# PSUM after the token loop: one rotating pool of four slots, against four one-slot pools with a written order in which the first and third slot change places

## The chip, the cores and the metric

The kernel runs on one core of a Trainium2 chip. The metric is device time in microseconds, the median of the timed runs. All time marks are microseconds from the first instruction of the profiled execution. Engines are named as in the profile: PE multiplies matrices, PEld is its weight load, DVE, ACT and POOL are the vector, scalar and GpSimd engines, and SP issues most of the DMAs.

## The reference

One transformer block on x of 2048 tokens by 640 values, in bfloat16: linear attention with a learned softmax feature map (32 heads of 20 values), then a gated feed-forward of width 1536.

```python
# _A_ref on layernorm(x)
phi_q = concat([softmax(pq), softmax(-pq)]);  phi_k = concat([softmax(pk), softmax(-pk)])
kv  = einsum("bhsf,bhsd->bhfd", phi_k, v);    z = einsum("bhsf->bhf", phi_k)
o   = einsum("bhqf,bhfd->bhqd", phi_q, kv) / (einsum("bhqf,bhf->bhq", phi_q, z) + 1e-6)
h   = x + o @ wo
# _B_ref on layernorm(h)
h2  = h + (gelu(hn @ w_gate) * (hn @ w_up)) @ w_down
```

## The kernel before

The 2048 tokens are 16 tiles of 128. The kernel has three stretches.

**The token loop** (`for t in range(NT)`, L463). For each tile PE makes keys and values, ACT takes exponentials, DVE and POOL normalise, and `kv_tile` (L345) adds the tile's part of the state into one PSUM tile, `kvp`. From the fourth tile on, PSUM has a pool of three two-bank slots (`psG`, L466) and a fourth two-bank slot for `kvp` (`psK`, L467). In the last turn of the loop `q_mm(0)` to `q_mm(3)` (L365) make the first four groups of queries, `q_exp` (L377) turns each into two exponentials on ACT, and the last `kv_tile` calls follow at L516 and L517. `kv_mask` (L356) then copies `kvp` into `KV` on DVE.

**The transition** (L518 to L802). The old pools are closed and `psG2` is opened at L523: one pool of four slots, each two banks of PSUM, so that slot 0 is banks 0 and 1, slot 1 is banks 2 and 3, slot 2 is banks 4 and 5, slot 3 is banks 6 and 7. Every PSUM tile of this stretch comes from it through `gtile` (L104) or, for the transposes on PE, straight from `transpose_to` (L152). The first calls are `q_mm(4, (0,))` (L758, five matmuls of the next query group), `attn_a(0, 1)` (L759, attention numerators and denominators of tile 0, two PSUM tiles `ab`), and so on. PE's and SP's order is the order of the calls, and so is that of the other engines (`manual_schedule`, L77 and L78).

**The feed-forward** (L805 to L829). `weave` (L739) runs the list of `gate_up` and `down` calls of one quarter of the tokens and puts stages of the remaining attention tiles between them. `gate_up` (L688) makes the gate and up products of 128 hidden columns in one two-bank tile `gu`; ACT takes the gelu of the first bank into `g` (L700), and DVE multiplies the second bank by it into `GT` (L703). `down` (L705) multiplies 12 such `GT` tiles by `Wd` into `pd` (L716), and DVE adds the residual into `y`. The first quarter is done in two halves. In the second half, at step 12 of the weave, that is after the twelfth `gate_up` and before the first `down`, `split()` (L543) closes `psG2` and opens `psB`, a pool of eight one-bank slots, which serves to the end.

A tile of a new pool may be written when all readers of the tiles that held its banks are done (`reuse_waits="tile"`). The waits are laid on PE's matmuls and weight loads.

Slots around the two borders, as the built program has them:

| tile | made at | slot before |
|---|---|---|
| query groups 0, 1, 2, 3, in the loop | L374 | 0, 2, 1, 0 (of the old pool) |
| kvp, in the loop | L352 | 3 (its own pool) |
| query group 4, first tile of `psG2` | L374 | 0 |
| the two `ab` tiles of attention tile 0 | L565 | 3, 2 |
| last `po` tile of `psG2` (attention tile 7) | L637 | 0 |
| `gu` of the tenth, eleventh and twelfth `gate_up`, the last tiles of `psG2` | L697 | 1, 3, 2 |
| first two tiles of `psB`, both `pd` | L716 | bank 0, bank 7 |

Of the kernel before, what the change touches and what calls it, by code (L numbers as in the profile page):

```python
# [8 lines left out]
BF16 = mybir.dt.bfloat16  # L9
F32 = mybir.dt.float32  # L10
# [3 lines left out]
PSUM = bass.MemoryType.PSUM  # L14
# [3 lines left out]
def kernel(  # L18
# [13 lines left out]
    P = 128  # L32
# [42 lines left out]
    ps_cm = ExitStack()  # L75
    psG = ps_cm.enter_context(tc.tile_pool(name="psG0", bufs=4, space=PSUM, reuse_waits="tile"))
# [24 lines left out]
    def small(pool, shape, name, bufs=3):  # L101
        return pool.tile(shape, F32, name=name, bufs=bufs)

    def gtile(name):  # L104
        return psG.tile([P, 2, 512], F32, name=name, tag="G")

    def ln_stats(pool, tiles, tag, act=True, between=None, log=False):

# [43 lines left out]
    def transpose_to(dst, src, on_pe, on_dve=False):  # L152

        if on_pe:
            tp = psG.tile([P, 16, P], BF16, name="tp", tag="G")
            for c in range(NC):
                nc.tensor.transpose(tp[:, c, :], src[:, c * P:(c + 1) * P], ident)  # L157
            (nc.vector.tensor_copy if on_dve else nc.scalar.copy)(dst, tp[:, 0:NC, :])  # L158
        else:
            nc.sync.dma_start_transpose(dst, src)  # L160
# [47 lines left out]
    for c in range(NC):  # L208
# [4 lines left out]
                                compare_op=ALU.is_ge, fill=0.0, base=Dh - 1 - off, channel_multiplier=-1)  # L213

    wu = gtile("wu")
    def warm(*cols):
        for n in cols:
# [4 lines left out]
    def fold(WT, W2, quarters, ds=range(NC)):  # L222


        n, w = (2, QF) if quarters else (1, HD)
        runs = []
        for c in range(NC):
            lo, hi = H0[c] * Dh, (H0[c] + NH[c]) * Dh
            for r in range(2 * n):
                a, b = max(lo, r * w), min(hi, (r + 1) * w)  # L230
                if a < b:
                    runs.append((r // n, r, c, a, b))
        runs.sort()
        for d in ds:
            wa = gtile("wa")
            wr = wa.rearrange("p u (q x) -> p (u q) x", q=n)
            for i, (u, r, c, a, b) in enumerate(runs):
                nc.tensor.matmul(wr[:, r, a - r * w:b - r * w], lhsT=WT[:, c, d * P:(d + 1) * P],
                                 rhs=BD[:, c].rearrange("p a b -> p (a b)")[:, a - H0[c] * Dh:b - H0[c] * Dh],
                                 start=(i == 0 or runs[i - 1][0] != u),  # L240
                                 stop=(i + 1 == len(runs) or runs[i + 1][0] != u), skip_group_check=True)
            dst, src = W2[:, d, :].rearrange("p (u f) -> p u f", u=2), wr[:, :, 0:w]
            if quarters:
                dst = W2[:, d, :].rearrange("p (c r f) -> p r c f", c=NC, r=4)
                src = src.rearrange("p r (c f) -> p r c f", c=NC)
            if d in (QA if quarters else KA):
                nc.scalar.copy(dst, src)
            else:
                nc.vector.tensor_copy(dst, src)
# [19 lines left out]
    def ln_ap(t, on_act=False, on_pe=False):  # L269
        ln = (ln_act if on_act else ln_dve)(p1, "1", *lnp[t])  # L270
        if on_pe:
            lnp[t] = ln
        else:
            transpose_to(LN1T[t // 4][:, :, t % 4 * P:(t % 4 + 1) * P], ln, False)

    def ln_tp(t, on_dve=False):
        transpose_to(LN1T[t // 4][:, :, t % 4 * P:(t % 4 + 1) * P], lnp[t], True, on_dve)
# [12 lines left out]
    def v_mm(t, us=(0, 1)):  # L290
        if 0 in us:
            pv[t] = gtile("pv")
        proj(pv[t], t, Wv, us)
# [120 lines left out]
    def tr_c(t):  # L414
        transpose_to(LN1T[0][:, :, t * P:(t + 1) * P], xc[t], True)
# [47 lines left out]
    for t in range(NT):  # L463
        if t == T3:
            ps_cm.close()
            psG = ps_cm.enter_context(tc.tile_pool(name="psG", bufs=3, space=PSUM, reuse_waits="tile"))  # L466
# [53 lines left out]
    p1_cm.__exit__(None, None, None)  # L520
    ps_cm.close()
    ps_cm = ExitStack()
    psG = ps_cm.enter_context(tc.tile_pool(name="psG2", bufs=4, space=PSUM, reuse_waits="tile"))  # L523


    p2 = ctx.enter_context(tc.tile_pool(name="p2", bufs=1, reuse_waits="tile"))
# [334 lines left out]
```

## Time and profile before

| | us |
|---|---|
| timed, median of 3 (lowest to highest) | 275.93 (275.52 to 276.19) |
| the profiled execution's own time | 276.65 |
| its span, first to last instruction | 274.7 |
| PE busy | 268.2 (98%) |
| PEld busy | 171.7 (63%) |
| DVE busy | 174.2 (63%) |
| ACT busy | 141.1 (51%) |
| POOL busy | 96.6 (35%) |

The granted clock of PE is 0.999 over the span. A row of the timeline gives the start, the length, the engine, the line, the operation, what it writes and reads, the shapes and how many instructions are merged into it; the bracket at its end is the time that the engine had nothing to run just before, and which instruction ended that. Matmuls overlap, so a row of several matmuls ends later than the next row begins. The chain of work that ended last is followed back from the last instruction, and PE has 73% of the span in it; it reaches back to 70.10 us.

### The profile page before, as it was taken

What the parts mean: (1) busy time and instruction counts of PE and PEld (TensorE: products, weight loads), DVE (VectorE), ACT (ScalarE), POOL (GpSimd) and SP (SyncE); (2) the same over time, 40 slices, a digit from 0 to 9 for tenths busy, and PEclk for the clock granted to TensorE, in tenths of its full rate; (3) what the DMA queues carried; (4) which work ended last, traced back from release to release, by engine and by line L of the source; (5) the groups of instructions that cost most, each with busy time, mean ns of one, the idle gap of its engine ahead of it and who ended that gap; (6) DMA issues with size and microseconds to landing.
All of it is one profiled execution on the core that took longest, in us unless ns stands there. A gap on an engine that the chain in (4) does not pass through costs nothing.

```text
span 274.7 us, 7230 instructions
## 1 busy us (share of the span) xinstructions
PE 268.2 (98%) x2978; PEld 171.7 (63%) x2995; DVE 174.2 (63%) x332; ACT 141.1 (51%) x241; POOL 96.6 (35%) x219
## 2 busy tenths in 40 slices
PE   7999999999899999999999999999999999999996
PEld 4776777774455887788754554675554576444574
DVE  5879999997586776675459873346976333333332
ACT  5789897787689755374534445212445510223100
POOL 4248999775012227365321552101165300000000
PEclk9999999999999999999999999999999999999999
DMA  7963637577079021323111232110214111000011
GB/s 190 221 218 71 66 60 91 78 152 312 2 246 328 5 50 37 85 51 73 33 43 49 26 70 51 40 58 1 66 32 64 35 48 50 24 0 0 2 48 48
DMA packets 42400, 21.46 MB, mean 78 GB/s; under 512 B 35200, under 2 KB 40576, under 8 KB 42368
## 3 DMA queue, kind: packets, MB, share of 16 engines
q1 hardware_dynamic: 41712, 20.98, 31.9%
q8 instruction: 23, 0.38, 0.6%
q10 hardware_dynamic: 656, 0.03, 0.2%
q14 instruction: 9, 0.07, 0.1%
HBM read 10.18 MB, written 2.62 MB: 47 GB/s over the span
## 4 chain that ended last, share of the span: by engine, by line
PE 73%; issue 0%; ACT 0%; DVE 0%
PE gu L697 38%; PE pd L716 19%; PE po L637 8%; PE pq L374 5%; PE ab L565 2%; PE tp L157 0%; ACT Eq L379 0%; DVE y L719 0%
## 5 line engine op out<-in xcount | busy, mean ns | idle before, releaser
L703 DVE TENSOR_TENSOR GT<-gu,g 128x512 bf16<-128x512 f32 (+1 forms) x60 | 34.4, 580 | 47.3 <-PE gu L697 38.5
L700 ACT ACTIVATE g<-gu 128x512 bf16<-128x512 f32 (+1 forms) x60 | 30.7, 512 | 63.6 <-PE gu L697 62.7
L697 PE MATMUL gu<-LN2T,Wg 128*128 128x512 bf16 (+1 forms) x289 | 61.2, 335 | 0.6
L697 PE MATMUL gu<-LN2T,Wu 128*128 128x512 bf16 (+1 forms) x300 | 61.8, 336 | 0.0
L716 PE MATMUL pd<-Wd,GT 128*128 128x320 bf16 (+2 forms) x396 | 53.5, 295 | 0.0
L716 PEld LDWEIGHTS <-GT 128*128 128x128 bf16 x396 | 37.9, 98 | 14.6 <-DVE GT L703 0.2
L697 PEld LDWEIGHTS <-Wu 128*128 128x128 bf16 x300 | 29.4, 98 | 22.6
L697 PEld LDWEIGHTS <-Wg 128*128 128x128 bf16 x300 | 28.6, 98 | 20.8
L285 PEld LDWEIGHTS <-LN1T 128*128 128x128 bf16 x290 | 27.7, 98 | 11.2 <-DMA LN1T<-ln 0.9
L719 DVE TENSOR_TENSOR y<-pd,x_sb 128x320 bf16<-128x320 f32 (+2 forms) x29 | 13.9, 480 | 29.4 <-PE pd L716 29.4
L333 POOL TENSOR_TENSOR vt<-vS,rs 128x672 bf16<-128x672 bf16 x22 | 29.2, 1349 | 7.5 <-DVE rs L329 7.2
L637 PE MATMUL po<-Wo,oT 128*128 128x320 bf16 x160 | 24.4, 299 | 0.0
L285 PE MATMUL pk<-Wk,LN1T 128*128 128x320 bf16 x160 | 24.2, 299 | 0.0
L374 PE MATMUL pq<-LN1T,Wq 128*128 128x512 bf16 x94 | 22.9, 379 | 1.2 <-ACT Eq L379 0.9
L325 DVE TENSOR_REDUCE sk<-E 128x64 f32<-128x1280 bf16 x16 | 22.9, 1430 | 0.0
L379 ACT ACTIVATE Eq<-pq 128x1024 bf16<-128x1024 f32 (+1 forms) x26 | 20.0, 828 | 3.3 <-PE pq L374 3.3
L285 PE MATMUL pv<-Wv,LN1T 128*128 128x320 bf16 x130 | 19.8, 299 | 0.4 <-DMA LN1T<-ln 0.3
L637 PEld LDWEIGHTS <-oT 128*128 128x128 bf16 x160 | 15.5, 98 | 7.0 <-ACT oT L158 0.5
L318 ACT ACTIVATE E<-pk 128x640 bf16<-128x640 f32 x28 | 18.2, 706 | 3.0 <-PE pk L285 2.9
L614 DVE TENSOR_TENSOR tt<-AB,w 128x1280 bf16<-128x1280 f32 x12 | 17.8, 1486 | 1.0 <-POOL w L607 0.9
L144 ACT ACTIVATE ln<-x_sb,v,rstd 128x640 bf16<-128x640 bf16 x14 | 12.9, 920 | 10.8 <-POOL v L676 10.3
L374 PEld LDWEIGHTS <-Wq 128*128 128x128 bf16 x100 | 9.4, 98 | 10.6 <-PE kvp L352 0.5
(114 smaller groups left out, 288.7 us busy)
## 6 DMA issues: line engine op xcount, KB each, us to landing
out_dram<-y SPq DMA_DIRECT2D x15, 160.0 KB, 1.8
Wg<-in_B_w_gate_dram SPq DMA_DIRECT2D x1, 1920.0 KB, 10.2
Wu<-in_B_w_up_dram SPq DMA_DIRECT2D x1, 1920.0 KB, 8.5
Wd<-in_B_w_down_dram SPq DMA_DIRECT2D x2, 960.0 KB, 11.8
x_sb<-in_A_x_dram SPq DMA_DIRECT2D x2, 640.0 KB, 6.5
Wo<-in_A_wo_dram SPq DMA_DIRECT2D x1, 800.0 KB, 5.6
x_sb<-in_A_x_dram SPq DMA_DIRECT2D x4, 160.0 KB, 3.4
Wv<-in_A_wqkv_dram SPq DMA_DIRECT2D x2, 320.0 KB, 4.5
```

The costliest lines, as they stand in the source:

```text
L285: nc.tensor.matmul(ps[:, u, 0:HD], lhsT=lnT(t, c), rhs=W[:, c, u * HD:(u + 1) * HD], start=(c == 0), stop=(c == NC - 1))
L318: nc.scalar.activation(Ek[t][:, s, :].rearrange("p (u f) -> p u f", u=2), pk[:, :, 0:HD], ACTF.Exp, scale=((lnp[t][2], nrstd[t]) if t in C ...
L325: nc.vector.reduce_sum(sk, Ek[t].rearrange("p s (h f) -> p (s h) f", f=Dh), axis=AX.X)
L333: eng.tensor_tensor(vt[:, s], vS[t % 8], rs[:, s * H:(s + 1) * H, None].to_broadcast([P, H, VC]), ALU.mult)
L374: nc.tensor.matmul(pqs[j][:, i, :], lhsT=Wq2[:, kc, c * P:(c + 1) * P], rhs=LN1T[b][:, kc, :], start=(kc == 0), stop=(kc == NC - 1))
L379: nc.scalar.activation(Eq[j][:, :, s, :], pqs[j][:, 0:len(QG[j])], ACTF.Exp, scale=(1.0, -1.0)[s])
L614: nc.vector.tensor_tensor(tt.rearrange("p s (h f) -> p s h f", f=Dh), num, w[:, :, :, None].to_broadcast([P, 2, H, Dh]), ALU.mult)
L637: nc.tensor.matmul(pos[u], lhsT=st[t][:, c, :], rhs=Wo[:, c, u * HD:(u + 1) * HD], start=(c == 0), stop=(c == NC - 1))
L697: nc.tensor.matmul(gu[i][:, 0:n], lhsT=W[:, c, f * P:(f + 1) * P], rhs=LN2T[b][:, c, a0:a1], start=(c == 0), stop=(c == NC - 1))
L700: nc.scalar.activation(g[:, 0:n], gu[0][:, 0:n], ACTF.Gelu_apprx_tanh)
L703: nc.vector.tensor_tensor(st[b, "g", f][:, a0:a1], gu[1][:, 0:n], g[:, 0:n], ALU.mult)
L716: nc.tensor.matmul(ps, lhsT=st[b, "g", f][:, tl * P:(tl + 1) * P], rhs=Wd[:, f, f0:f1], start=(f == 0), stop=(f == NF - 1))
```

## The change

The pool `psG2` is replaced by four pools of one two-bank slot each, and the list `ROT` says from which of them each tile of the stretch comes, in the order of the calls. Two helper lines follow from it: `gtile` takes the next number off the list while the four pools exist, and the transposes go through `gtile` as well.

```diff
+    psP = None
+
-    def gtile(name):
-        return psG.tile([P, 2, 512], F32, name=name, tag="G")
+    def gtile(name, shape=[P, 2, 512], dt=F32):
+        return (psP[ROT.pop(0)] if psP else psG).tile(shape, dt, name=name, tag="G")
...
-            tp = psG.tile([P, 16, P], BF16, name="tp", tag="G")
+            tp = gtile("tp", [P, 16, P], BF16)
...
-    psG = ps_cm.enter_context(tc.tile_pool(name="psG2", bufs=4, space=PSUM, reuse_waits="tile"))
+    psP = [ps_cm.enter_context(tc.tile_pool(name=f"psP{i}", bufs=1, space=PSUM, reuse_waits="tile")) for i in range(4)]
+    ROT = [2, 3, 0, 1, 3, 0, 2, 3, 0, 3, 1, 3, 1, 2, 0, 3, 1, 0, 2, 3, 0,
+           1, 2, 3, 0, 1, 2, 0, 1, 3, 2, 0, 1, 2, 3, 0, 1, 2, 3, 0, 1, 2,
+           3, 0, 1, 3, 0, 2, 1, 3, 0, 2, 1, 3, 0, 2, 1, 3, 0, 2, 1, 3, 0]
```

In the built program the list has 63 entries for 63 tiles. Each tile that had slot 0 now has slot 2, each that had slot 2 now has slot 0, and slots 1 and 3 keep theirs. The eight-bank pool behind the split, and all tiles before the transition, keep their banks. No engine gains, loses or moves an instruction.

## The prediction

> **What bounds the kernel.** I read the page first: PE is busy 268.2 of 274.7 us (98%). Then the chain that ended last: nothing but PE from about 70 us to the end, and ahead of PE one ACT row. Then the list of waits, for what PE itself waits for behind 60 us.
>
> ```profile
> PE 73%; issue 0%; ACT 0%; DVE 0%
> ```
> ```profile
> PE pq L374 <- ACT Eq L379: 0.9, 1, 0.9
> ...
> PEld L374 <- PE kvp L352: 0.5, 1, 0.5
> ```
>
> The reader is to see that PE is the bound, that it has a single wait of size on a PSUM slot behind the loop (0.9 us, on the exponentials `Eq`), and that a weight load just ahead of it was late by 0.5 us for another reason. So the tiles' places in PSUM are worth only what PE waits for them: a saved wait of PE is a gain that nothing takes back, since PE's matmuls have no other wait on an engine from there to the end, and an added one is a loss that nothing absorbs.
>
> **What the change moves.** It adds no instruction and moves none. Inside the stretch slots 0 and 2 only exchange their names: which tile follows which in one slot stays as it was, so all waits inside stay too. Comparing the two built programs wait by wait bears that out: DVE, POOL and SP have the same waits, ACT only signals at another place, and PE differs in a few waits at two borders. At the entry, query group 4 moves from the slot of group 3 to that of group 1, and the second `ab` tile takes the slot of group 3. At the exit, bank 0 was last used by a `po` tile and is now last used by the twelfth `gu`, and the first `pd` goes into bank 0. So there are two terms.
>
> **Entry: the wait on group 3 goes.** These rows of the timeline show it.
>
> ```profile
> 62.07 1.14 PE L352 MATMUL kvp<-vt,E 128*32 128x42 bf16 x120
> 65.51 1.94 ACT L379 ACTIVATE Eq<-pq 128x1024 bf16<-128x1024 f32 x2 [1.40 <-PE pq L374]
> 67.67 2.92 ACT L379 ACTIVATE Eq<-pq 128x1024 bf16<-128x1024 f32 x4 [0.22 <-PE pq L374]
> 68.64 1.14 PE L352 MATMUL kvp<-vt,E 128*32 128x42 bf16 x120
> 70.09 0.68 DVE L360 TENSOR_TENSOR KV<-kvp,kmask 128x504 bf16<-128x504 f32 x1
> 70.23 0.10 PEld L374 LDWEIGHTS <-Wq 128*128 128x128 bf16 x1 [0.55 <-PE kvp L352]
> 70.64 1.24 PE L374 MATMUL pq<-LN1T,Wq 128*128 128x512 bf16 x4 [0.86 <-ACT Eq L379]
> 71.81 0.47 PE L565 MATMUL ab<-KV,Eq 32*128 32x44 bf16 x40
> 75.55 0.47 PE L565 MATMUL ab<-KV,Eq 32*128 32x44 bf16 x40
> 75.95 2.33 PE L374 MATMUL pq<-LN1T,Wq 128*128 128x512 bf16 x9
> ```
>
> `kvp` ends at 68.64 + 1.14 = 69.78. The four exponentials of groups 2 and 3 end at 67.67 + 2.92 = 70.59, and 0.05 later, at 70.64, group 4 starts. After the change it needs group 1's exponentials, done at 65.51 + 1.94 = 67.45: no wait. But the matmul also needs its weights, and their load began only at 70.23. In both programs that load's only semaphore is PE's own count at the end of an earlier query group (group 3 before, group 1 after), and PE was through with both before `kvp` began. So no semaphore explains 70.23. What would be normal? After the first `kvp` run, which ended at 63.21, and after the second `ab` run, which ended at 76.02, the query matmuls began 0.07 before the modelled end (the load at 75.95, for one). By that rule group 4 could start at 69.78 - 0.07 = 69.71. The bounds of the gain are therefore 70.64 - 69.71 = **0.93** and 70.64 - 70.23 = **0.41** (and zero, if the late load gets later). I take 0.41: the change doesn't touch anything ahead of 69.8, so what held the load at 70.23 should hold it again.
>
> What could hold it? The page counts 23 instruction packets of 0.38 MB in all on queue q8, and PE has 2978 + 2995 instructions, so some 260 to a packet; the trace has one of these packets from 67.54 to 68.63 and the next at 71.35. The `kvp` run spends 240 instructions (120 loads, 120 matmuls) in 1.14 us, where a query matmul and its load take 0.22. So PE eats nearly a packet in the time that one packet travels.
>
> [...]
>
> Does the gain stay? The `ab` matmuls follow 1.17 behind group 4's start (71.81 - 70.64), at 71.40, or 70.88 at the earliest; `KV` is done at 70.77, and group 3's exponentials, which the second `ab` tile now waits for, at 70.59. Both are in time. From there ACT, DVE and POOL work on what PE gives them (all three stood idle for it about 72: DVE's and ACT's next rows are the copies of `ab`), so they shift with PE. The load of `Wu` starts behind group 4's exponential and shifts too.
>
> **Exit: a wait on the twelfth `gu` comes.**
>
> ```profile
> 132.92 0.71 PE L697 MATMUL gu<-LN2T,Wu 128*128 128x256 bf16 x5
> 133.35 0.76 ACT L700 ACTIVATE g<-gu 128x256 bf16<-128x256 f32 x2
> 133.46 3.42 PE L716 MATMUL pd<-Wd,GT 128*128 128x320 bf16 x24
> 133.75 0.81 DVE L703 TENSOR_TENSOR GT<-gu,g 128x256 bf16<-128x256 f32 x2 [1.37 <-ACT g L700]
> ```
>
> The twelfth `gu` ends at 132.92 + 0.71 = 133.63, ACT's gelu of it at 133.35 + 0.76 = 134.11, DVE's product at 133.75 + 0.81 = 134.56. `pd` starts at 133.46, in the overlap with the last `gu`, and goes on without a stop: the loads of its last three `GT` tiles had their own waits on DVE, and the twelfth, due 11 matmuls of 0.136 later (134.96 for the matmul), came after 134.56 and waited for nothing. After the change the first matmul of `pd` carries the wait for that same product (in the built program the three later waits are gone, covered by it). With the 0.05 seen above from release to start, `pd` starts at 134.61, so it costs 134.61 - 133.46 = **1.15**. Both bounds are near: gelu and product of one 256-column half take 0.38 and 0.42 with three hand-overs, so 133.63 + 0.80 + 0.05 to 0.15 makes at least 134.48 (1.02), and if ACT is late with it, as with the `ln` and `sq` that it ran just before, a few tenths more (1.4). Behind the waiting matmul stands all of PE's work: `pd`, the `ab` of tile 8 and the second quarter's `gu`. Whoever waits for those is later by as much. PE waits nowhere behind this, so nothing gives it back.
>
> **Sum.** 1.15 - 0.41 = +0.74 us. On the profiled execution's 276.65 (1.95 of it outside the span) that is 277.39. That execution is 0.72 above the median of the timed runs, 275.93, and what is timed is to be compared with the median: 275.93 + 0.74 = **276.67**, or 0.27% more. A measurement of this kernel can tell about 0.2% (0.55 us) from no change.
>
> **Rivals.**
> 1. *The late weight load goes with the wait* (not slower). Place: the load at 70.23. If it was late only because the matmul behind it waited, group 4 starts at 69.71, the entry gives 0.93, and the sum is +0.22: 276.15, no difference that can be told. For it: no semaphore explains the delay, and the 0.5 is seen once. Against it: another load ahead of a waiting matmul was not held (the load at 6.17, its matmul at 6.57). It decides from a start of group 4 ahead of about 70.04, where the sum falls under 0.55.
> 2. *The entry gives nothing*, because the weight load, or what feeds it, comes at 70.6 anyway: +1.15, 277.08. For it: the load is unexplained and may vary from run to run. Against it: a waiting load needs a cause, and none is added.
> 3. *The sum is wrong in a place that I don't see*, with the work of ACT and DVE meshing better behind the transition, or the kernel no different but in names. Against: the two waits are in the built program, and PE has no other wait to save. From -0.6 to +0.6.
>
> **Chances.** The forecast 0.58, rival 1 0.20, rival 2 0.12, rival 3 0.10. By the spread of the runs shown (0.67 us) I split each into slower by over 0.2%, within, faster: forecast 0.435, 0.139, 0.006; rival 1 0.03, 0.15, 0.02; rival 2 0.114, 0.006, 0; rival 3 0.05, 0.03, 0.02. That makes slower 0.63, same 0.32, faster 0.05. The range for 8 in 10 goes from rival 1 less the spread's half (276.15 - 0.25 = 275.9) to rival 2 and a little more (277.2).
>
> **What would show it.** In the changed kernel's profile the wait of `pq` on `Eq` is gone from PE's list; the first load of group 4 stands at 70.2 (forecast), 69.7 (rival 1) or 70.6 (rival 2), its matmul right behind it. PE has a new wait of about 1.1 us, `pd` on `GT` at DVE's L703, near 133 to 135, and PE's rows behind it are later than before by the sum. I am wrong if that wait isn't there, if PE has further waits between 72 and 133 us, or if the rows from 90 to 133 are not early by what group 4 gained.

## The result, and the profile after

| | before | after |
|---|---|---|
| timed, median (lowest to highest), 22 runs each | 276.15 (275.52 to 277.37) | 277.14 (276.24 to 278.41) |
| the profiled execution's own time | 276.65 | 276.36 |
| its span | 274.7 | 274.4 |
| PE busy | 268.2 (98%) | 268.6 (98%) |

The ratio of after to before is 1.0033, 95% interval 1.0021 to 1.0045: 0.91 us slower (0.58 to 1.24 of 276.15). The ratio is not that of the two medians, which are 0.99 apart. The forecast was 0.74 slower.

The two profiled executions seem to say the reverse, 274.4 after against 274.7 before. One span doesn't settle 0.3%: before, PE's list of waits had 0.5 us on the DMA of `Wv`, 0.3 on one of `LN1T` and 0.2 on `xc`, all within the first 50 us, where the change does nothing; after, none of the three is there. The last `kvp` run begins at 67.88 after, at 68.64 before. What the change does must be read from the border itself. This is PE's own list of waits after the change (the lines of the changed kernel are numbered 2 higher up to `psP`, 5 higher behind it: L374 is L376, L716 is L721):

```profile
PE pd L721 <- DVE GT L708: 1.0, 1, 1.0
PE wu L220 <- PEq L850: 0.8, 1, 0.8
PE pq L376 <- PE kvp L354: 0.2, 1, 0.2
```

The wait of `pq` on `Eq` is gone, and a wait of `pd` on `GT` stands in its place; what is left at `pq` (0.2) is on no other engine. The timeline of the entry:

```profile
66.91 2.92 ACT L381 ACTIVATE Eq<-pq 128x1024 bf16<-128x1024 f32 x4 [0.22 <-PE pq L376]
67.88 1.14 PE L354 MATMUL kvp<-vt,E 128*32 128x42 bf16 x120
69.19 0.76 PEld L376 LDWEIGHTS <-Wq 128*128 128x128 bf16 x5 [0.27 <-PE kvp L354]
69.19 1.25 PE L376 MATMUL pq<-LN1T,Wq 128*128 128x512 bf16 x4 [0.17 <-PE kvp L354]
70.38 0.30 PEld L570 LDWEIGHTS <-Eq 32*128 32x128 bf16 x33 [0.42 <-DVE KV L362]
```

`kvp` ends at 69.02 and the exponentials at 69.83. With the old slots group 4 would have started 0.05 behind those, at 69.88; it starts at 69.19. In this execution the entry gave 0.69. The first weight load is late here too: its place without a delay is 0.07 ahead of the end of `kvp`, at 68.95, and 69.19 - 68.95 = 0.24. The timeline of the exit:

```profile
131.48 0.71 PE L702 MATMUL gu<-LN2T,Wu 128*128 128x256 bf16 x5
131.91 0.76 ACT L705 ACTIVATE g<-gu 128x256 bf16<-128x256 f32 x2
132.31 0.81 DVE L708 TENSOR_TENSOR GT<-gu,g 128x256 bf16<-128x256 f32 x2 [1.37 <-ACT g L705]
133.18 3.42 PE L721 MATMUL pd<-Wd,GT 128*128 128x320 bf16 x24 [0.99 <-DVE GT L708]
```

The last `gu` ends at 132.19. Without a wait `pd` would start 0.16 ahead of that, as before (133.46 against 133.63), at 132.03; it starts at 133.18, 0.06 behind the end of DVE's product (133.12): 1.15 lost. Ahead of this point and behind it nothing moved: from group 4's first matmul to the end of the twelfth `gu` it is 62.99 before and 63.00 after, and from the first `pd` to PE's last matmul 138.55 in both.

### The profile page after: what moved, and what is told of

It reads as the page before. It is cut to its first block, busy times and chain, and to the rows that moved or that the text cites. A ratio compares the mean times of both kernels' runs of the same rounds, so it can differ in the third digit from the quotient of the medians.

```text
span 274.4 us, 7230 instructions
## 1 busy us (share of the span) xinstructions
PE 268.6 (98%) x2978; PEld 172.2 (63%) x2995; DVE 174.1 (63%) x332; ACT 140.8 (51%) x241; POOL 96.3 (35%) x219
## 4 chain that ended last, share of the span: by engine, by line
PE 95%; DVE 1%; ACT 1%; DMA 1%; issue 1%; ACTq 0%
PE gu L702 37%; PE pd L721 19%; PE po L642 8%; PE pk L287 8%; PE pq L376 8%; PE pv L287 7%; PE ab L570 2%; PE kvp L354 2%; PE tp L159 1%; PE wa L240 1%; DMA x_sb<-in_A_x_dram 1%; PE pv L303 1%; ACT vS L307 1%; ACT ln L146 0%; DVE statsc L116 0%
## 5 line engine op out<-in xcount | busy, mean ns | idle before, releaser
L721 PE MATMUL pd<-Wd,GT 128*128 128x320 bf16 (+2 forms) x396 | 53.5, 295 | 1.0 <-DVE GT L708 1.0
L721 PEld LDWEIGHTS <-GT 128*128 128x128 bf16 x396 | 37.9, 98 | 15.7 <-issue 1.2
L376 PE MATMUL pq<-LN1T,Wq 128*128 128x512 bf16 x94 | 22.9, 379 | 0.5 <-PE kvp L354 0.2
L376 PEld LDWEIGHTS <-Wq 128*128 128x128 bf16 x100 | 9.3, 98 | 10.0 <-PE kvp L354 0.3
```

Of the source, the lines that this page charges most:

```text
L376: nc.tensor.matmul(pqs[j][:, i, :], lhsT=Wq2[:, kc, c * P:(c + 1) * P], rhs=LN1T[b][:, kc, :], start=(kc == 0), stop=(kc == NC - 1))
L721: nc.tensor.matmul(ps, lhsT=st[b, "g", f][:, tl * P:(tl + 1) * P], rhs=Wd[:, f, f0:f1], start=(f == 0), stop=(f == NF - 1))
```

## The experiments

All times are against the kernel before, run on the same chip beside them. The table says what each run gave; the ratio need not be that of the two medians. "Load" is where the first weight load of group 4 stands behind the end of `kvp` in that kernel's one profile, "group 4" the same for its first matmul; -0.07 is the place without a delay. For kernels with one execution the ratio is left out.

| kernel | time | before beside it | ratio (95% interval) | load | group 4 |
|---|---|---|---|---|---|
| names_only | 276.27 | 276.39 | 1.0003 (0.9992 to 1.0014) | 0.75 | 0.86 |
| entry_only | 276.63 | 276.39 | 1.0008 (0.9988 to 1.0027) | 0.50 | 0.50 |
| exit_only | 277.39 | 276.39 | 1.0051 (1.0031 to 1.0070) | 0.53 | 0.86 |
| exit_gu11 | 277.01 | 276.52 | 1.0028 (1.0007 to 1.0049) | 0.59 | 0.86 |
| before_short_warm | 276.20 | 276.27 | 0.9993 (0.9980 to 1.0006) | -0.07 | 0.86 |
| after_short_warm | 276.42 | 276.27 | 1.0006 (0.9994 to 1.0019) | -0.07 | -0.07 |
| entry_short_warm | 275.38 | 276.39 | 0.9963 (0.9951 to 0.9975) | -0.07 | -0.07 |
| before_late_wg | 276.45 | 276.58 | 0.9999 (0.9980 to 1.0017) | -0.07 | 0.86 |
| entry_late_wg_timed | 275.48 | 276.58 | 0.9967 (0.9950 to 0.9984) | -0.07 | -0.07 |
| entry_late_wg | 274.71 | 276.52 | | -0.07 | -0.07 |
| entry_six_more | 276.48 | 276.27 | | -0.07 | -0.07 |
| entry_long_warm | 282.33 | 276.27 | | -0.07 | -0.07 |

### The two halves of the change, each alone, and neither

My theory: the sum of an entry gain, bounded by a late weight load, and an exit wait of 1.15. Its rivals: the load goes with the wait (0.93 gained), or the entry gives nothing. `entry_only` has the exchanged slots for the first 46 tiles and the old ones for the last 17. This and all later diffs show the lines that matter, against the changed kernel where no other is named.

```diff
-           3, 0, 1, 3, 0, 2, 1, 3, 0, 2, 1, 3, 0, 2, 1, 3, 0, 2, 1, 3, 0]
+           3, 0, 1, 3, 2, 0, 1, 3, 2, 0, 1, 3, 2, 0, 1, 3, 2, 0, 1, 3, 2]
```

> The entry of the change without its exit: the first 46 tiles behind the loop take the exchanged slots, the last 17 the slots of before. Theory (two terms, entry gain and exit wait): PE's wait of pq on Eq is gone, pd has no wait on GT at the split, and the time is below before by 0.4 to 0.7 us (0.15% to 0.25%), by how late the first weight load of query group 4 is (0.52 us in the profile of before, 0.24 in that of the change). Rival 1 (the late load goes with the wait): 0.93 us below, the load within 0.1 us of the end of kvp. Rival 2 (the entry gives nothing): the same as before.

`exit_only` is the opposite (the old numbers first, 0 and 2 exchanged for the last 17 tiles):

```diff
-    ROT = [2, 3, 0, 1, 3, 0, 2, 3, 0, 3, 1, 3, 1, 2, 0, 3, 1, 0, 2, 3, 0,
+    ROT = [0, 3, 2, 1, 3, 2, 0, 3, 2, 3, 1, 3, 1, 0, 2, 3, 1, 2, 0, 3, 2,
...
-           3, 0, 1, 3, 0, 2, 1, 3, 0, 2, 1, 3, 0, 2, 1, 3, 0, 2, 1, 3, 0]
+           3, 2, 1, 3, 0, 2, 1, 3, 0, 2, 1, 3, 0, 2, 1, 3, 0, 2, 1, 3, 0]
```

> The exit of the change without its entry: the first 46 tiles keep the slots of before, the last 17 take the exchanged ones. Theory: PE waits for Eq at the entry as before (0.86 us), and for GT at the first pd behind the split; the start of pd is 1.15 us behind where the overlap with the last gu would put it, and the time is 1.15 us above before (0.42%). A rival in which work on other engines takes the wait back: below 0.6 us, with PE rows behind the split that had waits and lose them.

`names_only` has four pools and the old slot for every tile (all 63 numbers with 0 and 2 exchanged back).

> Four one-slot pools with a list that gives every tile the slot of before: the same waits on all engines. Theory: the time of before within the measurement (0.2%). A rival in which four pools by themselves cost or gain: a difference beyond that. It also gives one more look at how late the first weight load of query group 4 is; if that is by chance, it varies from profile to profile between 0 and 0.9 us behind the end of kvp.

Measured: `names_only` 1.0003, so the pools by themselves do nothing that can be told (0.9992 to 1.0014). `exit_only` 1.41 us above (0.86 to 1.93), which holds 1.15, and in its profile `pd` starts 0.99 behind the modelled end of `gu` (132.47 + 0.71), as in the changed kernel:

```profile
132.47 0.71 PE L702 MATMUL gu<-LN2T,Wu 128*128 128x256 bf16 x5
134.17 1.11 PE L721 MATMUL pd<-Wd,GT 128*128 128x320 bf16 x7 [0.99 <-DVE GT L708]
```

`entry_only` is a miss in its time: 0.4 to 0.7 below was expected, measured is 0.22 above with an interval of -0.33 to 0.75. That is no difference that can be told from before, and the whole of the expected range lies outside the interval. Its profile shows what was meant: the wait on `Eq` is gone, and group 4 starts as soon as its weight load does, 0.36 ahead of where the old slots would have let it (the exponentials end at 67.22 + 2.92 = 70.14).

```profile
67.22 2.92 ACT L381 ACTIVATE Eq<-pq 128x1024 bf16<-128x1024 f32 x4 [0.22 <-PE pq L376]
69.83 0.76 PEld L376 LDWEIGHTS <-Wq 128*128 128x128 bf16 x5 [0.60 <-PE kvp L354]
69.83 1.04 PE L376 MATMUL pq<-LN1T,Wq 128*128 128x512 bf16 x4 [0.50 <-PE kvp L354]
```

Rival 1 falls: the wait is gone and the load is late all the same, in this kernel by 0.50 + 0.07, in the changed one by 0.17 + 0.07. The load is late by 0.24 to 0.82 in the six profiles of kernels that have before's dummy matmuls and early `Wg`. By these profiles the entry would give 0.93 less that lateness: 0.69 (after), 0.41 (before), 0.36, 0.33, 0.27 and 0.10, on average 0.36. That is an estimate from the places of the loads; the time of `entry_only` doesn't bear it out.

### The price of the exit, by the gu it waits for

`exit_gu11` keeps the slots of before for the first 41 tiles and exchanges 0 and 3 from the 42nd on, so that the first `pd` waits for the eleventh `gu` in place of the twelfth (the list's second and third rows are shown; tile 42 is the 3 at the end of the second):

```diff
...
-           1, 2, 3, 0, 1, 2, 0, 1, 3, 2, 0, 1, 2, 3, 0, 1, 2, 3, 0, 1, 2,
-           3, 0, 1, 3, 0, 2, 1, 3, 0, 2, 1, 3, 0, 2, 1, 3, 0, 2, 1, 3, 0]
...
+           1, 0, 3, 2, 1, 0, 2, 1, 3, 0, 2, 1, 0, 3, 2, 1, 0, 3, 2, 1, 3,
+           0, 2, 1, 0, 2, 3, 1, 0, 2, 3, 1, 0, 2, 3, 1, 0, 2, 3, 1, 0, 2]
```

> Like exit_only, but slots 0 and 3 change places from the 42nd tile on, so that the first pd waits for the eleventh gu and not the twelfth. Theory (the price is the end of DVE's product of that gu plus 0.05, less the start in the overlap): in the profile of before the eleventh product ends at 134.18, so pd starts 0.77 us behind its place without a wait (0.60 behind the modelled end of gu, where exit_only has 0.99), and the time is 0.77 us (0.28%) above before. Rival (any wait at the split costs a fixed restart of 1.0 to 1.4 us): as exit_only, 0.99 behind the end of gu.

```profile
132.62 0.71 PE L702 MATMUL gu<-LN2T,Wu 128*128 128x256 bf16 x5
133.93 0.84 PE L721 MATMUL pd<-Wd,GT 128*128 128x320 bf16 x5 [0.60 <-DVE GT L708]
```

`gu` ends at 133.33 and `pd` starts 0.60 behind it, where `exit_only` has 0.99. The time is 0.77 us above before (0.19 to 1.35), which by itself doesn't tell 0.77 from 1.15; the profiles do. So the wait costs what the named product takes, and no fixed restart.

### What holds the weight load of group 4

My theory: PE's instructions reach it by DMA in packets of some 260 (in the profile of before 2978 + 2995 instructions in 23 packets on queue q8), and the one that begins with this load is late. Rival: the load, its wait or the matmul behind it is slow by itself. PE has dummy matmuls on constants in the first 5 us (`warm`). `entry_short_warm` is `entry_only` with these in another cut: 9 in place of 15, so that every later PE instruction stands 12 places earlier (each dummy is a load and a matmul); the number of columns, 4608, stays.

```diff
-    warm(*[512] * 7, *[P] * 8)
+    warm(*[512] * 9)
```

> entry_only, with the dummy matmuls ahead of the first tile in another cut: nine of 512 columns in place of seven of 512 and eight of 128, the same number of columns with 12 PE instructions less, so that all later PE instructions stand 12 places earlier in their stream. If the first weight load of query group 4 is late because PE's sequencer waits for a packet of instructions that begins about there, it is late no more, or at another instruction: group 4 starts 0.07 us ahead of the end of kvp, 0.93 us earlier than before, and the time is 0.9 us (0.33%) below before. If it is late for a reason of its own (its wait, or the wait of the matmul behind it), nothing changes against entry_only.

```profile
68.56 1.14 PE L354 MATMUL kvp<-vt,E 128*32 128x42 bf16 x120
69.63 0.76 PEld L376 LDWEIGHTS <-Wq 128*128 128x128 bf16 x5
```

The load is on time, 0.07 ahead of the end of `kvp` (69.70), group 4's first matmul starts with it, and the kernel is 1.02 us below before (0.69 to 1.35). To see whether the short cut is worth that alone, the same line in the kernel before and in the changed one:

> The kernel before with the dummy matmuls cut as nine of 512 columns (12 PE instructions less ahead of everything). Theory (a late packet of instructions held group 4's first weight load, and the wait on Eq covered that): the load stands at the end of kvp, but its matmul still waits 0.86 us for Eq, so the time is that of before within 0.2%, or lower by 0.1 to 0.2 us where the load was at times later than Eq. Rival (the new cut is worth the 1.0 us by itself, wherever): 275.4, a full 0.33% below before, as entry_short_warm.

> The changed kernel with the same short cut. Theory: the entry gives its full 0.93 us and the exit costs 1.15, so +0.2 us against before (same within 0.2%), and 1.15 us above entry_short_warm: about 276.5 where that had 275.38. Rival (the two have nothing to do with each other): 0.9 us above before_short_warm, as the change is above before.

```profile
69.31 0.10 PEld L374 LDWEIGHTS <-Wq 128*128 128x128 bf16 x1
...
70.24 0.59 PE L374 MATMUL pq<-LN1T,Wq 128*128 128x512 bf16 x2 [0.86 <-ACT Eq L379]
```

These rows are of `before_short_warm`: the load is on time there too, but its matmul waits for `Eq` as ever, and the time is that of before (0.9993). With both short cut and new slots, `after_short_warm`, the two terms are 0.93 and 1.15, and the kernel is at 1.0006. `before_short_warm` was expected 0.93 above `entry_short_warm`, `after_short_warm` 1.15. They were run in another round, so they are compared by their ratios to before: 0.9993 and 1.0006 against 0.9963 make 0.83 and 1.19 above.

Two kernels put the border of the packet elsewhere. Both have the slots of `entry_only`. `entry_six_more` has `warm(*[512] * 6, *[P] * 12)`, 6 instructions more than `entry_only`, `entry_long_warm` has `warm(*[P] * 36)`, 42 more.

> entry_only with six of 512 columns and twelve of 128: 6 PE instructions more than entry_only ahead of everything. If the packet of instructions began at the first weight load of group 4, it now begins 6 instructions ahead of it, inside the last kvp run: a gap of 0.2 to 0.8 us between the weight loads of kvp, three loads before its end, and none between kvp and group 4. Rival (the load itself is late): a kvp run without a gap and the load 0.2 to 0.8 us behind its end.

> entry_only with 36 dummy matmuls of 128 columns: 42 PE instructions more ahead of everything, the same number of columns. By the packet theory the last packet begins 21 loads before the end of the last kvp run: a gap there, or none if the packet, asked for earlier, is in time; group 4 starts 0.07 us ahead of the end of kvp. Rival: the load late as in entry_only.

The weight loads of `entry_six_more`:

```profile
62.95 2.70 PEld L376 LDWEIGHTS <-Wq 128*128 128x128 bf16 x14
66.67 2.06 PEld L376 LDWEIGHTS <-Wq 128*128 128x128 bf16 x11 [1.01 <-issue]
69.14 1.07 PEld L354 LDWEIGHTS <-E 128*32 128x32 bf16 x120 [0.42 <-issue]
70.25 0.76 PEld L376 LDWEIGHTS <-Wq 128*128 128x128 bf16 x5
```

Group 4's load is on time (`kvp` ends at 70.32). The expected gap inside `kvp` is at the expected load, the 118th of 120, but small: 0.054 from one load's start to the next, where no two others are over 0.021 apart. The large gap came elsewhere, and at a place that says more: 1.01 us, 11 + 117 = 128 loads ahead of that one, which with their matmuls are 256 instructions. It is the border of the packet before. In `entry_long_warm`:

```profile
62.74 1.01 PEld L354 LDWEIGHTS <-E 128*32 128x32 bf16 x117 [0.42 <-issue]
66.75 0.10 PEld L354 LDWEIGHTS <-E 128*32 128x32 bf16 x3 [2.99 <-issue]
66.90 0.13 PEld L376 LDWEIGHTS <-Wq 128*128 128x128 bf16 x2
67.31 0.15 PEld L376 LDWEIGHTS <-Wq 128*128 128x128 bf16 x1 [0.28 <-issue]
```

A stop of 3 us in the middle of the first `kvp` run, with no semaphore in sight, at the 118th load once more. The gap was expected in the second run; it is one packet earlier.

Last, what makes the packet late. `entry_late_wg` has the slots of `entry_only`, keeps every PE instruction at its place and holds the load of `Wg` back until the exponentials of group 3 are done (the list isn't shown):

```diff
-            nc.sync.dma_start(Wg, wg_v)
...
+    nc.gpsimd.tensor_copy(Wg[:, 0, 0:1], Eq[3][:, 0, 1, 0:1])
+    nc.sync.dma_start(Wg, wg_v)
     q_mm(q, (0,))
```

> entry_only with the load of Wg (1.9 MB, from 57.8 us on in entry_only) held back until the exponentials of group 3 are done, near 70 us. Theory (the packet of instructions is late because the DMA engines are full with Wg): the two packets ahead of group 4 come earlier, and its first weight load stands 0.07 us ahead of the end of kvp, with the same PE instructions and the same places in their stream up to there as entry_only. Rival (crossing into a new packet costs PE 0.2 to 0.8 us anyway): the load as late as in entry_only. The time says little, since Wg, Wu and Wd then come together, and gate_up may wait for them.

The busy time by stretch, of the kernel before and then of `entry_late_wg`; the last three columns are PE's clock, the DMA engines' share and GB/s:

```profile
63.50:69.00 5.50, 5.45 (x72) 2.52 (x71) 3.60 (x5) 3.88 (x5) 3.28 (x2) 1.00 0.67 262
```
```profile
63.50:69.00 5.50, 5.50 (x142) 2.92 (x141) 2.50 (x4) 4.01 (x5) 2.44 (x2) 1.00 0.02 3
```

`entry_only`, which has the same PE instructions as `entry_late_wg`, stands at a share of 0.56 and 214 GB/s there (`after` at 0.48 and 187). With the DMA engines at a share of 0.02, the trace's records have the packet ahead of group 4 from 64.59 to 65.94 in place of 67.17 to 68.30 in `entry_only`, and the load stands at its place without a delay (`kvp` ends at 69.04):

```profile
67.90 1.14 PE L354 MATMUL kvp<-vt,E 128*32 128x42 bf16 x120
68.96 0.76 PEld L376 LDWEIGHTS <-Wq 128*128 128x128 bf16 x5
```

Timed, with the same edit in the kernel before beside it:

> The kernel of entry_late_wg once more, now timed. Theory: with the packets of instructions in time the entry gives its whole 0.93 us and no exit wait stands against it: 0.9 to 1.8 us below before (0.33% to 0.65%); its one execution so far was 1.8 below.

> The kernel before with the load of Wg held back in the same way, and the slots as they were. Theory: PE still waits 0.86 us for Eq at group 4, so it lies 0.93 us above entry_late_wg_timed, and at or a few tenths below before, as far as a late packet cost anything beyond the wait. Rival (the late Wg load alone is the gain): as entry_late_wg_timed.

The first is 0.91 us below before (0.44 to 1.38), the second at 0.9999: 0.97 between them, where 0.93 was expected. The late `Wg` alone is worth nothing that can be told, the new entry slots alone nothing either, both together 0.9. The rival is out, and both this kernel and `entry_short_warm` beat the two kernels of the case.

## Why the prediction was right, step by step

**PE is the bound, and only its waits count.** Held. The span falls into three pieces, and outside the two borders they don't change: from the first `pd` to PE's last matmul 138.55 in before, after, `exit_only`, `exit_gu11`; from group 4's start to the first `pd` 62.81 to 62.84 wherever the exit is the old one, 63.98 to 63.99 wherever it is the new one.

**Inside the stretch the exchange is only of names.** Held: no wait of PE between 72 and 133 us in any of these profiles beyond those of before, and `names_only` is at 1.0003.

**Entry, 0.41 of at most 0.93.** The mechanism was right: the wait on `Eq` went, and the late weight load became what group 4 starts with. The size was taken from one execution, and the six profiles have 0.10 to 0.69, on average 0.36. So 0.41 was no lower bound, as the prediction had it (four of the six lie below), and that it came near the mean is luck. No time shows it: the measured 0.91 less the exit's 1.15 leaves an entry gain of 0.24, with an interval of -0.09 to 0.57, and `entry_only` has at most 0.33. The gain may be smaller still outside of the profiled executions (the 12 of `entry_only` went from 274.93 to 278.55, where before beside it had 275.97 to 277.13). Each execution that is timed has no trace of its own here, so how late the packet was in those stays open.

**What holds the load.** The prediction asked the question and answered from packet size and issue rate; shown now by moving the border (group 4's load 0.07 ahead of the end of `kvp` in all three kernels with the short cut, 0.24 to 0.82 later in the six with before's dummy matmuls and early `Wg`), and by emptying the DMA engines (a share of 0.02, and the load on time, in `entry_late_wg`). Two borders are 128 loads apart in `entry_six_more`, with their matmuls 256 instructions. `kvp` takes 4.8 ns per instruction (240 in 1.14 us); with the DMA engines busy for 0.48 (`after`), 0.67 (before) and 0.94 (`entry_long_warm`) of the stretch ahead of their start (63.5 to 69, in the last 60 to 66.7), PE's loads were held there for 0.24, 0.52 and 2.99 us.

**Exit, 1.15.** Right within 0.02 in three profiles (132.03 to 133.18 after; from group 4 to `pd` 62.82 before, 63.98 in `exit_only`, 63.99 in `after_short_warm`), and it follows the product that is waited for: 0.77 expected and 0.77 found for the eleventh.

**The sum.** 0.74 forecast, 0.91 measured (0.58 to 1.24); with the six profiles' mean for the entry it would be 1.15 - 0.36 = 0.79. Rival 1 (+0.22) is what `after_short_warm` shows once the packet is in time (1.0006), but it isn't what the change does; rival 2 (the entry gives nothing, +1.15) lies inside the interval of the time, fits the time of `entry_only` too, and is spoken against by the profiles alone, where group 4 started 0.69 and 0.36 early. So the sum came out by a sure exit term and an entry term whose size stays open.

## What to carry to other kernels

In this kernel, where PE is busy for 98% of the span, the new order of buffers was worth only the difference of PE's waits at the borders of the pools (in the profiles 0.69 gained, 1.15 lost). So where one engine bounds a kernel, list its waits one by one in both programs and price each by the end of the reader that it names. The wait that was removed here, 0.86 us on `Eq`, uncovered a weight load that was late by 0.24 to 0.82: look at the weight load ahead of the waiting matmul, not at the matmul alone. And a gain found at one border need not be bought with a loss at the other: the list could change over at a place that brings PE no wait, as `entry_only` does at the 47th tile (in its time that showed only once the packet was out of the way, as in `entry_short_warm` and `entry_late_wg_timed`).

## What the runs showed of the hardware that was not expected

Around the runs of tiny matmuls (`kvp`: 240 PE instructions in 1.14 us) PE stood still at the border of an instruction packet where the load of `Wg` (1920 KB, 10.2 us from issue to landing before) had filled the DMA engines ahead of it (before, a share of 0.92 from 57 to 63.5 us and 0.67 from there to 69): with `Wg` loaded there a packet came late in eight of eleven profiles, with `Wg` held back in none of three. In the eight held borders PE went on 1.36 to 1.60 us after the end of the packet in the DMA records (68.63 to 70.23 before, 67.72 to 69.19 after, 65.29 to 66.75 in `entry_long_warm`), and the next packet started 1.1 to 1.4 us after the held load where that was group 4's. What passes in those 1.4 us isn't settled.

With the new entry slots, twelve instructions less in the first 5 us went with 1.25 us less time: 275.38 with nine dummy matmuls, 276.63 with fifteen, 282.33 in the one execution with 36. That last loss is larger than its stop: PE's granted clock fell to half in it, at 66.01 by the trace's clock record, and came back at 72.84, as the stretches of `entry_long_warm` show in the column ahead of the last two.

```profile
66.70:73.00 6.30, 6.25 (x19) 2.29 (x19) 0.24 (x1) 1.61 (x2) 1.42 (x1) 0.51 0.25 95
73.00:90.00 17.00, 17.00 (x285) 9.12 (x283) 10.37 (x22) 13.61 (x18) 1.57 (x3) 1.00 0.42 144
```

In this one execution the pause between matmuls was 2.9 us (63.86 to 66.75); the clock fell 2.15 us into it and was at half for 6.8 us, 6.1 of them behind the pause. The pauses of 0.86 us (before, at the entry) and 0.99 us (after, at the exit) left the clock at 1.00 (69 to 71.7 before, 132 to 134 after). What sets either length isn't shown.
